# A new written order, new loads and new PSUM banks for an attention + ELU feed-forward kernel; the first pair's q and k transposed as fp32

## The chip, the cores and the metric

The kernel runs on one core of one Trainium2 chip, in one launch. The time is the device time of that core in microseconds (us), as the median of several executions. The core has five engines that run side by side and wait for each other through semaphores: TensorE (PE, matmuls; PEld is its weight load), VectorE (DVE), ScalarE (ACT), GpSimd (POOL) and SyncE (SP). Transfers between memory and the core are issued by POOL, SP and ACT into queues.

## The reference

Attention over 8 batches of 8 heads, 576 positions, 64 dimensions, and behind it a feed-forward block with ELU over all 4608 tokens:

```python
scores = scale * np.matmul(q, k.transpose(0, 1, 3, 2))
mask_local = (rel >= 0) & (rel < stride)                  # stride = 32, rel = i - j
mask_strided = (rel >= 0) & (pos[None, :] % stride == pos[:, None] % stride)
masks = np.stack([mask_local if h < H // 2 else mask_strided for h in range(H)], axis=0)
attn = softmax(np.where(masks, scores, -1e9))             # over the last axis
x = (attn @ v) as 4608 tokens x 512                       # 8 heads x 64 beside each other
h = x @ w_in                                              # 512 -> 2048
g = np.where(h > 0, h, np.exp(np.minimum(h, 0)) - 1)
return g @ w_out                                          # 2048 -> 512, fp32
```

Heads 0 to 3 are local, heads 4 to 7 strided. Inputs and output are fp32 in memory; the matmuls run in bf16.

## The kernel before, in words

The work of each engine follows one text, `ORDER` (line 36), in which each word is one step. A loop at the end of the kernel reads the words and calls the function of each; every engine then works through its own steps in the order of the text and waits only where a semaphore says so. The words:

- `w.bank.n.n...` (`warm`, L385): matmuls on zeros with n columns each, into a bank whose content is not needed. They keep TensorE busy where it would wait.
- `D.x.b` (`load`): a load, issued by POOL. `qs`, `ks`, `vs` are the strided heads of batch b, `ql`, `kl`, `vl` the local ones, `wi0` to `wi3` the quarters of w_in (4 of 16 blocks m of 128 hidden columns each), `wo0` to `wo3` those of w_out. Loads convert to bf16. From the ninth load on, each one waits until the eighth before it has landed, because eight semaphores are reused in turn.
- `K`, `k` (`cast`, L390): half of the first strided pair's q or k from fp32 to bf16. This pair comes through SP's and ACT's queues instead of POOL's, as fp32, into a staging space that lies in `g`.
- `T` (`transposes`, L401, L408, L411): q or k of a pair of heads of batch 0 or 1 is transposed by TensorE into a PSUM bank; `c` (VectorE) or `C` (ScalarE) (`copy_T`) copies it out. A pair is named by batch, kind and number: `0s0` is the first strided pair of batch 0, `1l1` the second local one of batch 1. For `0s0` the transpose goes in halves, `.0` and `.1`.
- `X` (`dma_T`, L601): from batch 2 on, q and k are transposed by a DMA that SP issues.
- `S` (`scores`, L453), `e` (`exp_s`, L460, ScalarE), `m` (`mask`, L467 and L473, VectorE), `O` (`pv`: values and row sums; L480 to L501 in an old form for batches 0 and 1, L516 and L523 in a new one from batch 2), `n` (logarithm of the sums, L551, ScalarE), `r` (exponential of its negative, L556, ScalarE), `x` (`write_x`, L581, VectorE: the product goes to `xT` as bf16): the attention steps of a pair's half.
- `V`, `W`: copies that bring v into the form that `O` reads. `F`: fills of masks and ones.
- `L.ch.m.bank` (L608): the first product for a chunk of 512 tokens and block m, four matmuls of 512 columns over the four blocks of 128 features. Features 0 to 255 come from local heads, 256 to 511 from strided ones. For chunk 0 it is split: `a` does the strided two, `b` the local two.
- `h` (exponential, L616, ScalarE), `i` (L625, VectorE) or `j` (L623, ScalarE) (the clamp), `g` (L636 or L634, VectorE): the ELU of a block; `g` reads the PSUM bank last, which is then free.
- `Z.ch.k.part.bank` (L642): a quarter of the second product of 128 tokens, four matmuls; `q` (VectorE) or `o` (ScalarE) copies the finished bank out (L648), and `t` stores it from SP's queue, `u` from SP's and ACT's in turn.
- `Y`, `y` (L672, L682): the last tile in three pieces, each stored as soon as it is ready.

PSUM has eight banks; the last number in a word that writes PSUM names them, so the text also fixes which step waits for which bank.

TensorE's front, before: zeros, transposes of `0s0` in halves as the casts finish, the other pairs' transposes, scores, PV, each with zeros between them; then four `a` of quarter 1 (blocks 5, 7, 4, 6), a transpose of batch 1 (`T.1s1.q`), and the `b` of these blocks. From there on the dense words of a chunk alternate with the attention words of a later batch. At the end only `Z` words are left.

Of the kernel before, what the change touches and what calls it, by code (L numbers as in the profile page):

```python
# [8 lines left out]
F32 = mybir.dt.float32  # L9
BF16 = mybir.dt.bfloat16  # L10
I32 = mybir.dt.int32
ALU = mybir.AluOpType
# [3 lines left out]
S = 576  # L16
# [24 lines left out]
D.wi2.0 c.0l0.q n.0s0.0 w.4.314 S.0l1.1.45 S.0l1.0.23 m.0s0.1 F.mk r.0s0.0 T.0l0.k.7 O.0s0.1.60 e.0l1.1  # L41
x.0s0.0 D.wo0.0 F.ml e.0l1.0 w.0.224.224.102 O.0s1.1.15 c.0l0.k n.0s0.1 D.wo1.0 w.4.247 O.0s1.0.43
n.0s1.1 m.0l1.0 n.0s1.0 r.0s1.1 D.ql.1 w.2.512.512.108 S.0l0.0.23 x.0s1.1 e.0l0.0 V.0 w.7.512.331
S.0l0.1.01 r.0s1.0 m.0l1.1 r.0s0.1 w.7.512 O.0l1.0.75 m.0l0.0 e.0l0.1 O.0l1.1.32 x.0s1.0 n.0l1.0 m.0l0.1
w.2.224.224 O.0l0.0.10 n.0l1.1 x.0s0.1 r.0l1.0 w.1.142 O.0l0.1.54 r.0l1.1 x.0l1.0 D.ks.1 n.0l0.0
w.4.224.224 a.0.5.6 x.0l1.1 n.0l0.1 a.0.7.7 r.0l0.0 a.0.4.0 r.0l0.1 x.0l0.0 a.0.6.4 D.kl.1 x.0l0.1
T.1s1.q.3 b.0.5 c.1s1.q b.0.7 h.0.5 b.0.4 h.0.7 i.0.5 b.0.6 h.0.4 g.0.5 T.1s0.q.5 D.wo2.0 a.0.12.3
C.1s0.q i.0.4 a.0.13.6 h.0.6 g.0.4 a.0.14.5 b.0.12 a.0.15.2 h.0.12 b.0.15 j.0.6 D.vs.1 a.0.2.1 j.0.12
b.0.13 g.0.6 b.0.2 h.0.13 g.0.12 a.0.1.4 h.0.2 i.0.7 b.0.1 i.0.13 a.0.3.3 g.0.7 h.0.1 D.wo3.0 b.0.3
i.0.2 b.0.14 h.0.3 g.0.2 a.0.0.7 j.0.1 b.0.0 a.0.11.1 g.0.1 h.0.0 a.0.10.0 h.0.14 D.vl.1 i.0.0 b.0.10  # L50
j.0.3 g.0.0 b.0.11 h.0.10 a.0.8.4 g.0.3 b.0.8 h.0.11 g.0.13 Z.0.0.0.7 h.0.15 i.0.10 D.ks.2 i.0.14
Z.0.0.1.7 h.0.8 g.0.10 j.0.11 Z.0.3.0.6 j.0.15 g.0.11 D.vs.2 Z.0.3.1.6 g.0.15 g.0.14 a.0.9.3 D.qs.2
i.0.8 b.0.9 g.0.8 Z.0.1.0.5 h.0.9 j.0.9 T.1s0.k.4 D.kl.2 Z.0.1.1.5 C.1s0.k g.0.9 T.1s1.k.2 S.1s0.1.01
c.1s1.k T.1l1.k.4 e.1s0.1 T.1l1.q.3 c.1l1.k T.1l0.q.2 S.1s1.0.01 m.1s0.1 Z.0.3.2.6 e.1s1.0 C.1l1.q
m.1s1.0 Z.0.1.2.5 C.1l0.q O.1s1.0.43 T.1l0.k.2 n.1s1.0 S.1s1.1.01 c.1l0.k Z.0.0.2.7 e.1s1.1 r.1s1.0
# [12 lines left out]
Z.1.2.1.2 n.2s0.1 x.2s1.1 Z.1.3.2.7 r.2s0.1 m.2s0.0 O.2s1.0.01 x.2s0.1 Z.1.2.2.2 n.2s1.0 O.2s0.0.34
r.2s1.0 Z.1.3.3.7 n.2s0.0 x.2s1.0 Z.1.2.3.2 r.2s0.0 q.1.3 S.2l0.0.01 S.2l0.1.56 x.2s0.0 Z.1.1.0.7
e.2l0.0 q.1.2 e.2l0.1 m.2l0.0 S.2l1.0.01 S.2l1.1.34 X.qs.3 Z.1.1.1.7 m.2l0.1 e.2l1.0 e.2l1.1 m.2l1.0  # L70
O.2l0.0.56 O.2l0.1.01 X.kl.3 n.2l0.0 m.2l1.1 Z.1.0.0.4 n.2l0.1 Z.1.0.1.4 r.2l0.0 t.1.3 O.2l1.1.23
r.2l0.1 x.2l0.0 Z.1.0.2.4 n.2l1.1 x.2l0.1 O.2l1.0.56 r.2l1.1 Z.1.0.3.4 X.ql.3 n.2l1.0 x.2l1.1 Z.1.1.2.7
r.2l1.0 D.qs.4 Z.1.1.3.7 x.2l1.0 D.kl.4 q.1.0 L.2.11.6 W.3 S.3s0.0.01 S.3s0.1.23 h.2.11 L.2.3.5 e.3s0.1
i.2.11 g.2.11 L.2.7.4 D.ks.4 h.2.3 o.1.1 D.vl.3 i.2.3 L.2.2.6 m.3s0.1 e.3s0.0 g.2.3 L.2.5.7 h.2.7 h.2.2
i.2.7 L.2.4.5 h.2.5 g.2.7 j.2.2 i.2.5 L.2.9.3 m.3s0.0 h.2.4 D.vs.4 g.2.5 L.2.0.4 h.2.9 g.2.2 j.2.4
D.ql.4 L.2.14.7 i.2.9 h.2.0 g.2.4 O.3s0.1.01 h.2.14 g.2.9 L.2.10.6 n.3s0.1 i.2.0 L.2.6.5 i.2.14 h.2.10
g.2.0 r.3s0.1 L.2.8.3 i.2.10 X.ks.4 g.2.14 h.2.6 L.2.13.4 x.3s0.1 h.2.8 j.2.6 g.2.10 O.3s0.0.01 X.qs.4
L.2.1.7 n.3s0.0 i.2.8 g.2.6 L.2.15.6 r.3s0.0 g.2.8 t.1.0 h.2.1 L.2.12.5 x.3s0.0 h.2.15 X.kl.4 i.2.1
S.3s1.0.01 S.3s1.1.23 g.2.1 e.3s1.1 Z.2.1.0.7 e.3s1.0 m.3s1.1 i.2.15 h.2.13 m.3s1.0 S.3l0.0.01
# [70 lines left out]
def kernel(  # L150
# [583 lines left out]
```

## Time and profile before

| | us |
|---|---|
| median of 3 runs (lowest to highest) | 305.96 (305.51 to 306.67) |
| the profiled execution, its own time | 306.22 |
| its span, first to last instruction | 304.5 |
| TensorE busy | 297.1 |
| ScalarE busy | 228.5 |
| VectorE busy | 226.2 |
| GpSimd busy | 80.2 |
| first dense matmul starts | 18.62 |

The granted clock of TensorE is 1.00 over the whole span. In the lines shown below, times count from the first instruction. A line of a timeline gives start, length, engine, line of the kernel, operation, what it writes and reads, how many are merged, and in brackets how long the engine was idle before and what ended that. The matmuls are pipelined, so the length of one is longer than the distance to the next.

### The profile page before, as it was taken

To read this page: it belongs to the slowest core of one execution; us is meant where nothing else is said; L and a number is where in the kernel's file an instruction comes from. 1 tells how busy PE (TensorE), PEld (TensorE's weight loads), DVE (VectorE), ACT (ScalarE), POOL (GpSimd) and SP (SyncE) were. 2 spreads that over 40 slices of the span, in tenths; PEclk is the share of its full clock that TensorE was granted. 3 is DMA by queue.
4 is the path that set the end of the run, shared out by engine and by line. 5 is a ranking of instruction groups with operands and counts; after the bars stand their busy time and mean duration, and the time that the engine had idled before them with its cause. 6 is when DMAs were issued, how large, how long until landed. Compare 5 with 4: busy or idle time off the path is not lost.

```text
span 304.5 us, 6258 instructions
## 1 busy us (share of the span) xinstructions
PE 297.1 (98%) x2339; PEld 146.8 (48%) x2339; DVE 226.2 (74%) x435; ACT 228.5 (75%) x412; POOL 80.2 (26%) x110
## 2 busy tenths in 40 slices
PE   6999999999999999999999999999999999999994
PEld 2654455445544454445544554445444544444444
DVE  6777968798779978896788878976788358895020
ACT  4778678598879888997989889978777559982101
POOL 8922436830471008530188250000000000000000
PEclk9999999999999999999999999999999999999999
DMA  8999999999899759999899499801120022000053
GB/s 165 190 206 207 207 193 169 169 198 204 158 158 168 128 123 134 162 192 171 196 154 154 61 132 149 195 16 56 38 69 0 2 69 69 2 1 0 4 155 119
DMA packets 107358, 37.63 MB, mean 124 GB/s; under 512 B 89152, under 2 KB 102848, under 8 KB 107328
## 3 DMA queue, kind: packets, MB, share of 16 engines
q0 software_dynamic: 69728, 19.47, 62.3%
q1 hardware_dynamic: 36920, 17.08, 28.4%
q10 hardware_dynamic: 680, 0.69, 0.8%
q8 instruction: 18, 0.29, 0.4%
q14 instruction: 12, 0.10, 0.1%
HBM read 39.53 MB, written 9.44 MB: 161 GB/s over the span
## 4 chain that ended last, share of the span: by engine, by line
PE 86%; DVE 6%; ACT 3%; issue 2%; DMA 2%; ACTq 0%; DVEq 0%
PE ps L642 40%; PE ps L608 33%; PE ps L453 4%; DVE g L636 3%; DVE he L625 2%; PE ps L523 2%; PE ps L516 2%; DMA g<-in_k_dram 2%; PE ps L385 1%; PE ps L672 1%; ACT he L616 1%; PE ps L411 1%; PE ps L496 1%; PE ps L480 1%; ACT ln L551 0%
## 5 line engine op out<-in xcount | busy, mean ns | idle before, releaser
L642 PE MATMUL ps<-w_out_sb,g 128*128 128x512 bf16 x560 | 132.8, 379 | 0.5 <-DVE g L636 0.5
L608 PE MATMUL ps<-xT,w_in_sb 128*128 128x512 bf16 x576 | 130.5, 379 | 0.2 <-DVE g L634 0.2
L616 ACT ACTIVATE he<-ps 128x512 f32<-128x512 f32 x144 | 80.9, 596 | 22.2 <-PE ps L608 20.0
L608 PEld LDWEIGHTS <-w_in_sb 128*128 128x128 bf16 x576 | 55.0, 98 | 64.3 <-issue 1.1
L642 PEld LDWEIGHTS <-g 128*128 128x128 bf16 x560 | 51.1, 98 | 55.7 <-issue 0.8
L636 DVE TENSOR_TENSOR g<-he,ps 128x512 bf16<-128x512 bf16 x92 | 62.0, 684 | 1.9
L581 DVE TENSOR_TENSOR xT<-ps,ln 64x576 bf16<-64x576 f32 (+1 forms) x64 | 42.6, 678 | 20.3 <-ACT ln L556 19.4
L460 ACT ACTIVATE e<-ps 72x576 bf16<-72x576 f32 (+1 forms) x64 | 39.1, 647 | 12.7 <-PE ps L453 11.9
L625 DVE TENSOR_SCALAR he<-he 128x512 bf16<-128x512 f32 x92 | 40.2, 446 | 7.5 <-ACT he L616 6.8
L551 ACT ACTIVATE ln<-ps 64x576 f32<-64x576 f32 (+1 forms) x64 | 36.3, 583 | 10.0 <-PE ps L523 5.0
L634 DVE SCALAR_TENSOR_TENSOR g<-he,ps 128x512 bf16<-128x512 bf16 x52 | 34.8, 682 | 7.2 <-ACT he L623 6.9
L556 ACT ACTIVATE ln<-ln 64x576 f32<-64x576 f32 (+1 forms) x64 | 38.5, 619 | 1.2
L623 ACT ACTIVATE he<-he 128x512 bf16<-128x512 f32 x52 | 32.5, 630 | 1.3 <-DVE g L636 0.8
L648 DVE COPY osb<-ps 128x512 f32<-128x512 f32 x22 | 15.1, 685 | 16.3 <-PE ps L642 16.0
L243 POOL DMA_DIRECT2D ql<-in_q_dram x24 | 20.1, 840 | 7.7 <-DMA vl<-in_v_dram 4.1
L648 ACT COPY osb<-ps 128x512 f32<-128x512 f32 x13 | 7.6, 586 | 17.9 <-PE ps L642 14.1
L250 POOL DMA_DIRECT2D kl<-in_k_dram x24 | 17.8, 747 | 11.4 <-DMA w_out_sb<-in_moe_w_out_dram 3.7
L473 DVE TENSOR_TENSOR pm<-e,mask_l 128x576 bf16<-128x576 bf16 x32 | 14.1, 453 | 6.9 <-ACT e L460 5.3
L467 DVE TENSOR_TENSOR pm<-e,mask_s 72x576 bf16<-72x576 bf16 x32 | 14.2, 451 | 4.3 <-ACT e L460 4.1
L260 POOL DMA_DIRECT2D vl<-in_v_dram x8 | 9.8, 1220 | 9.5 <-PE ps L523 7.2
L233 POOL DMA_DIRECT2D vs<-in_v_dram x8 | 5.2, 652 | 25.6 <-DVE vsp L588 24.7
L516 PEld LDWEIGHTS <-vsp 72*128 72x128 bf16 x192 | 9.1, 98 | 5.5 <-issue 0.4
(93 smaller groups left out, 153.2 us busy)
## 6 DMA issues: line engine op xcount, KB each, us to landing
out_dram<-osb SPq DMA_DIRECT2D x30, 144.0 KB
vl<-in_v_dram POOLq DMA_DIRECT2D x8, 288.0 KB, 8.9
w_in_sb<-in_moe_w_in_dram POOLq DMA_DIRECT2D x4, 512.0 KB, 13.1
w_out_sb<-in_moe_w_out_dram POOLq DMA_DIRECT2D x4, 512.0 KB, 16.8
kl<-in_k_dram POOLq DMA_DIRECT2D x24, 72.0 KB, 7.3
ql<-in_q_dram POOLq DMA_DIRECT2D x24, 72.0 KB, 8.4
ks<-in_k_dram POOLq DMA_DIRECT2D x5, 320.0 KB, 8.2
vs<-in_v_dram POOLq DMA_DIRECT2D x5, 320.0 KB, 9.1
```

The lines of the kernel that those rows point to most:

```text
L460: nc.scalar.activation(e[0:R], tiles.pop(("S", key, u))[0:R], ACT.Exp, scale=scale)
L551: nc.scalar.activation(t, s_ps, ACT.Ln)
L556: nc.scalar.activation(t, t, ACT.Exp, scale=-1.0)
L581: nc.vector.tensor_mul(dst, o_ps, rc)
L608: nc.tensor.matmul(tiles["h", ch, m], lhsT=w_in_sb[:, c, m * 128:(m + 1) * 128], rhs=xT[:, c, ch * CHUNK:(ch + 1) * CHUNK], start=(c == 2) ...
L616: nc.scalar.activation(e, tiles["h", i[0], i[1]], ACT.Exp)
L623: nc.scalar.activation(e1, e, ACT.Relu, bias=1.0, scale=-1.0)
L625: eng.tensor_scalar(e1, e, scalar1=1.0, scalar2=1.0, op0=ALU.min, op1=ALU.subtract)
L634: nc.vector.scalar_tensor_tensor(dst, e1, -1.0, h, op0=ALU.mult, op1=ALU.max)
L636: nc.vector.tensor_tensor(dst, e1, h, op=ALU.max)
L642: nc.tensor.matmul(ops, lhsT=g[ch % 2][:, m, kk * 128:(kk + 1) * 128], rhs=w_out_sb[:, m, :], start=(m == 0), stop=(m == MC - 1), skip_gro ...
L648: eng(o_sb, tiles.pop(("o", int(ch), int(kk))))
```

## The change

The order text is written anew: other places for nearly all words, other banks, other blocks first, and another split of copies and clamps between VectorE and ScalarE at single places (18 `q` and 17 `o` for 22 and 13 before, while 92 `i` and 52 `j` stay). The code changes with it in these points:

- The casts `K` and `k` are gone. The halves of pair `0s0` are transposed straight from the fp32 staging space, with a second identity in fp32 (72 x 72), into PSUM as fp32; the copy out of PSUM converts.
- The scores of `0s0` load 72 weight columns instead of 128.
- `load` can take a quarter of w_in in two halves; the new text does not use it.
- In front, the order of loads behind the first pair is kl, kl, ql, ql, vs, vs, vl, then w_in quarters 3, 0, 2, 1, then qs of batch 1, w_out 0, ks of batch 1, and so on. Before, it was ql, kl, ql, vs, kl, vs, vl, w_in 1, qs of batch 1, w_in 3, 0, 2.
- For batch 2, ql (four loads) is loaded ahead of qs and kl.
- O of `0l0.0` comes after the first two `a`. Five `a` (blocks 15, 12, 14, 13, 1) stand before the first `b`.
- Chunk 6's second product is spread between the first products of chunks 7 and 8.
- One late tile is stored from two queues (`u.8.2`), where there were two (`u.8.3`, `u.7.2`).

```diff
-w.7.512.512.512.512.512.512.512.512 D.ql.0.1 F.vp D.kl.0.1 F.v1 D.ql.0.0 k.q.0 F.ms D.vs.0.0 T.0s0.q.0.7
-D.kl.0.0 K.q.1 K.k.1 D.vs.0.1 K.k.0 C.0s0.q.0 w.0.512.512.512.512.512 T.0s0.k.0.6 D.vl.0 T.0s0.k.1.5
-T.0s0.q.1.4 c.0s0.k.0 T.0s1.k.7 c.0s0.k.1 c.0s1.k w.0.324 T.0s1.q.6 c.0s0.q.1 D.wi1.0 S.0s0.0.01 c.0s1.q
-S.0s0.1.23 e.0s0.0 w.5.185 S.0s1.0.45 D.qs.1 S.0s1.1.67 e.0s1.0 m.0s0.0 w.2.224.224 T.0l1.k.1 D.wi3.0
-e.0s1.1 m.0s1.0 w.0.499 T.0l0.q.0 C.0l1.k D.wi0.0 m.0s1.1 T.0l1.q.7 e.0s0.1 c.0l1.q w.4.155 O.0s0.0.16
...
+w.7.512.512.512.512.512.512.512.512 D.kl.0.1 F.vp D.kl.0.0 F.ms D.ql.0.1 F.v1 D.ql.0.0 T.0s0.q.0.7
+D.vs.0.1 T.0s0.k.0.6 c.0s0.q.0 D.vs.0.0 C.0s0.k.0 D.vl.0 w.0.512.512.512.512.512.394 T.0s1.k.7
+T.0s0.q.1.6 c.0s1.k S.0s0.0.01 c.0s0.q.1 e.0s0.0 w.2.269 T.0s1.q.5 D.wi3.0 T.0s0.k.1.7 C.0s1.q m.0s0.0
+w.2.421 T.0l1.k.6 c.0s0.k.1 D.wi0.0 S.0s1.1.01 C.0l1.k S.0s1.0.23 S.0s0.1.45 D.wi2.0 T.0l0.k.7 e.0s1.1
+w.2.123 T.0l1.q.6 e.0s1.0 D.wi1.0 m.0s1.1 e.0s0.1 w.0.224.224.182 T.0l0.q.1 m.0s1.0 D.qs.1 c.0l0.k
+C.0l1.q w.0.512.132 O.0s1.1.05 F.mk O.0s1.0.43 n.0s1.1 S.0l1.0.67 D.wo0.0 F.ml e.0l1.0 w.2.198
...
+m.0l1.1 r.0s0.1 n.0l1.0 w.4.224.224.105 O.0l1.1.51 x.0s0.1 n.0l0.1 m.0l0.0 D.wo2.0 n.0l1.1 a.0.15.6
+r.0l1.1 a.0.12.3 r.0l1.0 x.0l1.1 O.0l0.0.21 r.0l0.1 x.0l1.0 a.0.14.0 n.0l0.0 x.0l0.1 a.0.13.7 r.0l0.0
+x.0l0.0 D.vs.1 a.0.1.1 b.0.15 b.0.12 b.0.13 h.0.12 b.0.1 h.0.13 a.0.0.2 h.0.15 D.wo3.0 a.0.2.5 i.0.13
...
+o.8.0 t.8.0 Z.8.1.3.2 Z.7.1.2.5 q.8.1 Z.7.1.3.5 t.8.1 Z.7.0.2.4 q.7.1 Z.7.0.3.4 t.7.1 Y.7.3.0.7 o.7.0
+t.7.0 y.7.3.0 Y.7.3.1.6 y.7.3.1 Y.7.3.2.5 y.7.3.2
...
+    identity_f = consts.tile([RS, RS], F32, tag="identity_f", name="identity_f")
...
-        if y is not None:
+        if y is not None and nm != "wi":
...
+            cs = slice(0, KC) if y is None else (slice(2, KC), slice(0, 2))[int(y)]
+            nc.gpsimd.dma_start(out=w_in_sb[:, cs, i * 512:(i + 1) * 512],
+                                in_=w_in_v[:, cs, i * 512:(i + 1) * 512])
...
+    nc.vector.memset(identity_f, 1.0)
...
+    nc.gpsimd.affine_select(
+        identity_f, identity_f, compare_op=ALU.is_equal, fill=0.0,
+        base=0, pattern=[[1, RS]], channel_multiplier=-1)
...
-    def cast(eng, nm, i):
-        n, f = "qk".index(nm), 2 * NS * D
-        eng(half(raw[nm + "s"][0:RS, 0:f], int(i)), half(stage[0:RS, n * f:(n + 1) * f], int(i)))
...
-        t = ps[:, bank, :].bitcast(BF16)[:, 0:S // (1 + len(part))]
+        t = ps[:, bank, 0:W] if part else ps[:, bank, :].bitcast(BF16)[:, 0:S]
...
+            n = "qk".index(nm) * 2 * NS * D
+            src = stage[0:RS, n:n + 2 * NS * D].rearrange("p (h f) -> p h f", h=2)
...
-                nc.tensor.transpose(t[:, i * RS:(i + 1) * RS], src[:, P.head(x), c0:c0 + 2 * D],
-                                    identity[0:RS, 0:RS])
+                nc.tensor.transpose(t[:, i * RS:(i + 1) * RS], src[:, x, c0:c0 + 2 * D], identity_f)
...
-                nc.tensor.matmul(dst, lhsT=P.kT[pr, k0:k0 + 128], rhs=rhs, start=True, stop=True,
+                n = RS if key == "0s0" else 128
+                nc.tensor.matmul(dst[0:n], lhsT=P.kT[pr, k0:k0 + n], rhs=rhs, start=True, stop=True,
...
```

More of the change, by code (lines that the diff above doesn't have):

```diff
@@ L41 @@
[L41 to L55, printed above, removed]
@@ L273, in load @@
             i = int(what[2])
-            nc.gpsimd.dma_start(out=w_in_sb[:, :, i * 512:(i + 1) * 512],
-                                in_=w_in_v[:, :, i * 512:(i + 1) * 512])
+            cs = slice(0, KC) if y is None else (slice(2, KC), slice(0, 2))[int(y)]
+            nc.gpsimd.dma_start(out=w_in_sb[:, cs, i * 512:(i + 1) * 512],
+                                in_=w_in_v[:, cs, i * 512:(i + 1) * 512])
         elif nm == "wo":
@@ L686 @@
     run = {
-        "w": warm, "K": lambda nm, x: cast(nc.vector.tensor_copy if nm == "q" else nc.scalar.copy, nm, x),
-        "k": lambda nm, x: cast(nc.scalar.copy if nm == "q" else nc.vector.tensor_copy, nm, x), "T": transposes, "F": fill,
+        "w": warm, "T": transposes, "F": fill,
         "c": lambda *a: copy_T(nc.vector.tensor_copy, *a),
```

189 lines of the change are left out of this document (99 added, 90 removed).

## The prediction

> **What bounds the kernel now.** I read the page first, then each engine's busy time in stretches of 10 us, then the timelines of the front by engine, then the chain of waits and the end. Columns of a group: busy us, mean ns of one, idle us before it.
>
> ```profile
> PE 297.1 (98%) x2339; PEld 146.8 (48%) x2339; DVE 226.2 (74%) x435; ACT 228.5 (75%) x412; POOL 80.2 (26%) x110
> ...
> L642 PE MATMUL ps<-w_out_sb,g 128*128 128x512 bf16 x560 | 132.8, 379 | 0.5 <-DVE g L636 0.5
> L608 PE MATMUL ps<-xT,w_in_sb 128*128 128x512 bf16 x576 | 130.5, 379 | 0.2 <-DVE g L634 0.2
> ...
> L608 PEld LDWEIGHTS <-w_in_sb 128*128 128x128 bf16 x576 | 55.0, 98 | 64.3 <-issue 1.1
> ```
>
> TensorE is the bound: it is busy 98% of the span, and its 1136 dense matmuls waited 0.7 us in all. So there are only three places where a new order can change the time: the front, before dense work runs; the few stalls inside; the end behind the last matmul.
>
> ```profile
> core 0 of [0], span 304.5 us
> core 0: us, PE busy (x) PEld busy (x) DVE busy (x) ACT busy (x) POOL busy (x), PEclk, DMA share, GB/s
> 60.00:70.00 10.00, 9.78 (x74) 4.49 (x73) 9.70 (x20) 9.24 (x19) 3.62 (x5) 1.00 1.57 193
> 90.00:100.00 10.00, 9.91 (x60) 4.72 (x59) 9.85 (x20) 9.51 (x18) 2.61 (x4) 1.00 1.80 168
> 100.00:110.00 10.00, 9.53 (x99) 4.89 (x97) 8.49 (x17) 9.07 (x17) 0.00 (x0) 1.00 0.46 95
> 150.00:160.00 10.00, 9.94 (x71) 4.42 (x69) 8.82 (x17) 8.32 (x16) 7.60 (x11) 1.00 1.08 152
> ```
>
> These four (with the length of each first) are the only stretches from 40 us to 300 us in which TensorE is under 10.00. They lack 0.22, 0.09, 0.47 and 0.06, so 0.84 us in all, and the three worst lie where VectorE is at 9.7 and 9.85 of 10, or just behind. All of the middle can yield 0.84 us and no more.
>
> ```profile
> 1.26 3.50 PE L385 MATMUL ps<-zero 128*128 128x512 bf16 x8 [1.26 <-DVE zero L303]
> 4.95 0.30 PE L401 MATMUL ps<-identity,qs 72*128 72x72 bf16 x4 [0.19 <-ACT qs L390]
> 5.09 1.25 PE L385 MATMUL ps<-zero 128*128 128x512 bf16 x5
> 7.26 0.43 PE L401 MATMUL ps<-identity,ks 72*128 72x72 bf16 x8 [0.92 <-ACT ks L390]
> ...
> 18.62 1.89 PE L608 MATMUL ps<-xT,w_in_sb 128*128 128x512 bf16 x8
> 20.35 0.42 PE L408 MATMUL ps<-identity,xT 72*128 72x72 bf16 x8
> 20.75 1.89 PE L608 MATMUL ps<-xT,w_in_sb 128*128 128x512 bf16 x8
> ```
>
> In this timeline of TensorE (start, length, instruction, idle before) the first dense matmul starts at 18.62. The 8 at 18.62 are first halves of chunk 0 (tokens `a`, strided heads), those at 20.75 begin the second halves (`b`, local heads). Up to there TensorE fills waits with matmuls on zeros, so it is ScalarE that sets the front:
>
> ```profile
> 8.76 0.65 ACT L460 ACTIVATE e<-ps 72x576 bf16<-72x576 f32 x1 [1.26 <-PE ps L453]
> 9.69 1.18 ACT L460 ACTIVATE e<-ps 72x576 bf16<-72x576 f32 x2 [0.28 <-PE ps L453]
> 10.76 0.63 ACT L429 COPY kTl<-ps 128x576 bf16<-128x576 bf16 x1
> 11.28 0.66 ACT L460 ACTIVATE e<-ps 72x576 bf16<-72x576 f32 x1
> ...
> 19.27 0.76 ACT L556 ACTIVATE ln<-ln 128x288 f32<-128x288 f32 x2
> ```
>
> Its first exponential is at 8.76, and its last reciprocal ends at 20.03; a multiply of 0.46 on VectorE then lets the `b` start at 20.75. One 576-wide instruction occupies 0.53 (10.76 less 9.69, halved). From the slot after the fourth exponential (11.28 + 0.55 = 11.83) to 20.03 stand 4 exponentials, 8 logarithms and 8 reciprocals, 8.20 us with little idle in them.
>
> **The change, part by part.** *No casts.* Three casts of ScalarE and one of VectorE go; the 16 transposes of the first pair read the fp32 loads. The 0.92 us that TensorE waited for a cast go too, but filler stands in their place: the columns of zeros are 12,946 for 12,903 before, by the order text, so TensorE's own time in front is as it was.
>
> *What a transpose in fp32 costs* no row shows. The row at 4.95, with the next start at 5.09, gives 0.035 each in bf16, the lower end. [...] I take 0.13, nearest to the two rows added, so 0.53 for a group of four. [...]
>
> *The front, worked through.* Zeros end at 4.76. Then q and k of half 0: 1.06, to 5.82; zeros of 2954 columns (5.77 matmuls at 0.216): 1.25, to 7.07. Then the transposes of the loaded `ks`:
>
> ```profile
> 2.13 0.64 POOL L233 DMA_DIRECT2D ks<-in_k_dram  x1
> ```
> ```profile
> ks<-in_k_dram POOLq DMA_DIRECT2D x1, 160.0 KB, 5.1
> ```
>
> The second row is the load's issue with its median time to landing: it lands at 2.13 + 5.1 = 7.23. So 0.26 to 7.50, q of half 1 to 8.03, the first scores (0.24, and 0.1 for the switch) to 8.37, and ScalarE's first exponential at 8.45, 0.3 sooner than 8.76. But the new order gives ScalarE three 576-wide copies between the exponentials (of q of pair 0s1, k and q of 0l1) where there was one. It copies until 9.5, waits for TensorE's k of half 1 and the transposes of 0l1 to 9.85, copies to 10.37, has three exponentials to 12.0 and the last copy to 12.53. The old 8.20 us follow: 20.73. With the multiply, the `b` start at 21.25. The new order has done five `a` by then instead of four and a transpose, 0.43 less 0.26, so 20.75 corresponds to 20.93: the front is 0.3 us later. With 0.035 a transpose ScalarE ends near 20.1 and the front is bounded by weights instead.
>
> *Weights in another order* (w_in quarters 3, 0, 2, 1, and qs of batch 1 behind them). POOL's loads wait for the eighth before them to land, so its rows give the landings:
>
> ```profile
> 17.86 0.64 POOL L233 DMA_DIRECT2D xT<-in_k_dram  x1 [2.95 <-DMA w_in_sb<-in_moe_w_in_dram]
> 19.46 0.64 POOL L233 DMA_DIRECT2D xT<-in_k_dram  x1 [0.96 <-DMA xT<-in_q_dram]
> 22.39 0.75 POOL L278 DMA_DIRECT2D w_out_sb<-in_moe_w_out_dram  x1 [2.29 <-DMA w_in_sb<-in_moe_w_in_dram]
> 24.54 0.65 POOL L233 DMA_DIRECT2D g<-in_v_dram  x1 [1.41 <-DMA w_in_sb<-in_moe_w_in_dram]
> 27.08 0.75 POOL L278 DMA_DIRECT2D w_out_sb<-in_moe_w_out_dram  x1 [1.89 <-DMA w_in_sb<-in_moe_w_in_dram]
> ```
>
> A quarter takes 2.15 to 2.93, so the second now lands at 17.86 plus that, 20.0 to 20.8. The fifth `a` needs it, so the `b` cannot start before 20.45 to 21.2. That holds the front between -0.5 and +0.3 even where ScalarE is early. The fourth quarter lands by 25.5; the first `a` that reads it stands 5.6 us behind the fifth, at 26: no wait, by half a microsecond.
>
> *Order in the middle.* The counts are the same (92 clamps on VectorE, 52 on ScalarE, 64 of each attention step); four PSUM copies go from VectorE to ScalarE. What a switch costs shows here, in the chain of waits:
>
> ```profile
> 75.49 1.73 PE ps L642 x8
> 77.22 0.36 PE ps L453 x12
> 77.58 0.97 PE ps L642 x4
> ```
>
> Four dense matmuls take 0.97 behind scores, where eight took 1.73 (0.86 for four): 0.1 on the way out, and about as much on the way in. By the order texts dense work now breaks off 35 times for scores, transposes or the old PV form, for 33 before: two more at 0.2, of which one only moves over from the front: +0.2. The stalls of 0.84 may go or double; stretches with VectorE near its limit stand in both orders (by token counts and row durations, about 9.4 and 9.9 us of work in 10 at the same two places, and a new one in chunk 6), so I take them as they are, 0, with -0.84 and +1.0 for the range. Bank reuse is no tighter: spans under 2.6 us from a first product to its bank's next use are 14 in both.
>
> *The end.*
>
> ```profile
> 300.66 0.29 DVE osb L682
> ```
>
> The last tile still goes out in pieces; the last 128-column copy and its store remain, from 300.66 to 304.5. One full tile before them goes through one queue instead of two, and is done well before: 0.
>
> *Sum.* +0.3 + 0.2 + 0 = +0.5 on 306.22 us, the time of the profiled execution (span 304.5, and 1.72 around it): 306.7. The median shown is 305.96, 0.26 lower, so 306.5 for the median.
>
> **The rivals.** [...]
>
> *Late loads* (slower). qs of batch 2 is now issued behind its four ql loads:
>
> ```profile
> 50.10 2.74 SPq L601 DMA_TRANSPOSE qTs<-qs  x1
> ```
> ```profile
> 64.49 0.44 PE L453 MATMUL ps<-qTs,kTs 64*128 64x72 bf16 x16
> ```
>
> That moves this transpose by about 2 us, to 52, and its scores from 64.5 to 62.3: the 14 us between them shrink to 10. Elsewhere TensorE's work between a transpose and its use comes to 11 us or more. If one of them, or a quarter of w_in, is over its margin by 1.5 to 3 us: 307.5 to 309. Against it: the queue's order is by need, and each margin is positive.
>
> *Clean* (faster). All 0.84 us of stalls go, quick transposes let ScalarE end near 19.9 and w_in lands at its fastest: -0.5, so -1.34: 304.6, just within 0.5%; a little off the end as well makes it faster. For it: nothing of the work grew. Against it: three mild gains at once.
>
> *No effect where it is meant*: the casts are gone, but copies take their room on ScalarE. That is the forecast itself.
>
> **How the numbers follow.** Under 0.5%, 1.5 us, this kernel's runs (305.51 to 306.67) hardly tell a change from none. Forecast 0.62 (306.5; its own range 305.4 to 307.4), slow transposes 0.13, late loads 0.12, clean 0.13, of which 0.11 over the bound. So faster 0.11, same 0.64, slower 0.25. The range reaches down past most of the clean case, 304.8, and up into the two slow ones, 308.3.
>
> **What would show it.** The fp32 transposes' start-to-start (0.13); the first exponential near 8.45; ScalarE's last reciprocal near 20.7; the `b` near 21.2; stretches below 10.00 in the middle that add up to about 0.8; the end from the last copy still 3.8. The prediction is wrong if TensorE waits on a DMA in the middle, or if the front moved by over a microsecond.

## The result, and the profile after

| | before | after |
|---|---|---|
| median of 14 runs each (lowest to highest) | 305.85 (305.51 to 306.67) | 306.86 (306.40 to 308.59) |
| the profiled execution, its own time | 306.22 | 306.81 |
| its span | 304.5 | 305.1 |
| second halves of chunk 0 (`b`) start | 20.75 (as 20.93 in the new order) | 21.92 |
| from the last copy to the end | 3.84 | 3.83 |

The ratio of after to before is 1.0037, with a 95% interval of 1.0027 to 1.0047: one microsecond slower. Before's profiled execution lay 0.37 over its kernel's median, after's 0.05 under its own, so the two profiles differ by only 0.6. Most line numbers move by 4 to 6: `L391` are the zeros, `L405` the fp32 transposes, `L457` the scores, `L612` and `L646` the dense products. Of casts_back, a run further down, two of the seven executions lie near 314 us and are left out of its ratio, and the profiled one is one of these two.

The page of after, its engines and the two dense groups:

```profile
PE 297.6 (98%) x2345; PEld 147.7 (48%) x2345; DVE 220.1 (72%) x429; ACT 231.7 (76%) x415; POOL 80.2 (26%) x111
...
L646 PE MATMUL ps<-w_out_sb,g 128*128 128x512 bf16 x560 | 134.1, 379 | 0.0
L612 PE MATMUL ps<-xT,w_in_sb 128*128 128x512 bf16 x576 | 131.8, 379 | 0.4
```

The dense products waited 0.4 us instead of 0.7. TensorE is as busy as before; VectorE has lost 6 us of work, ScalarE has gained 3. After in stretches of 10 us, the only four below 10.00 between 40 and 300:

```profile
core 0: us, PE busy (x) PEld busy (x) DVE busy (x) ACT busy (x) POOL busy (x), PEclk, DMA share, GB/s
...
50.00:60.00 10.00, 9.76 (x76) 4.76 (x74) 7.58 (x18) 7.39 (x17) 1.46 (x3) 1.00 2.01 135
...
100.00:110.00 10.00, 9.94 (x99) 5.11 (x100) 8.60 (x18) 8.22 (x15) 0.00 (x0) 1.00 1.35 198
110.00:120.00 10.00, 9.84 (x81) 4.99 (x80) 6.31 (x10) 9.01 (x15) 3.61 (x5) 1.00 0.39 71
...
160.00:170.00 10.00, 9.85 (x80) 4.71 (x78) 9.85 (x20) 9.23 (x17) 5.00 (x7) 1.00 2.21 154
```

They lack 0.61 us, where before lacked 0.84. The end is unchanged: the last copy (timeline of VectorE in after) starts 3.83 before the span's end.

```profile
301.27 0.29 DVE L686 COPY osb<-ps 128x128 f32<-128x128 f32 x1 [0.55 <-PE ps L676]
```

So the loss lies in the front. After's timeline of TensorE:

```profile
4.46 0.67 PE L405 MATMUL ps<-identity_f,g 72*128 72x72 f32 x8
4.97 1.41 PE L391 MATMUL ps<-zero 128*128 128x512 bf16 x6
7.22 0.43 PE L411 MATMUL ps<-identity,ks 72*128 72x72 bf16 x8 [0.84 <-DMA ks<-in_k_dram]
7.49 0.45 PE L405 MATMUL ps<-identity_f,g 72*128 72x72 f32 x4
7.87 0.33 PE L457 MATMUL ps<-qTs,kTs 64*72 64x72 bf16 x8
...
15.76 0.22 PE L457 MATMUL ps<-qTl,kTl 64*128 64x96 bf16 x2
16.82 0.26 PE L457 MATMUL ps<-qTl,kTl 64*128 64x96 bf16 x4 [0.84 <-issue]
17.01 0.35 PE L391 MATMUL ps<-zero 128*128 128x224 bf16 x2
...
20.38 6.88 PE L612 MATMUL ps<-xT,w_in_sb 128*128 128x512 bf16 x30
```

Three things are to be seen. Eight fp32 transposes take 4.97 less 4.46, so 0.064 each. The wait for a cast (0.92 us) is gone, and a wait of nearly the same length for the load of `ks` (0.84) stands in its place. And at 15.98, in the middle of the scores of `0l0.0`, TensorE stands still for 0.84 us "<-issue", that is, for nothing that the profile shows: two of the six matmuls of this step had run, and the program has no wait between them.

ScalarE in after, from its first exponential to its last reciprocal of batch 0:

```profile
8.24 0.65 ACT L464 ACTIVATE e<-ps 72x576 bf16<-72x576 f32 x1 [2.67 <-PE ps L457]
...
11.81 0.62 ACT L428 COPY qTl<-ps 128x576 bf16<-128x576 bf16 x1
12.46 0.41 ACT L555 ACTIVATE ln<-ps 128x288 f32<-128x288 f32 x1
13.13 0.65 ACT L464 ACTIVATE e<-ps 128x576 bf16<-128x576 f32 x1 [0.25 <-DVE mask_l L360]
...
17.40 0.65 ACT L464 ACTIVATE e<-ps 128x576 bf16<-128x576 f32 x1 [0.52 <-DVE xT L585]
...
20.49 0.41 ACT L555 ACTIVATE ln<-ps 128x288 f32<-128x288 f32 x1
20.93 0.44 ACT L560 ACTIVATE ln<-ln 128x288 f32<-128x288 f32 x1
```

It starts 0.5 sooner than before (8.76) and ends 1.3 later (20.03). The last exponential, at 17.40, comes 0.04 us behind the end of the two zero matmuls that stand behind the scores of `0l0.0` (17.01 and 0.35 long, so 17.36), which go to the free columns of a bank that these scores use. It is so in casts_zeros, too (zeros to 17.09, exponential at 17.13), while in no_late_fill, which leaves these zeros out, it comes 0.04 behind the scores themselves (17.49 and 17.53). So it seems to wait for the zeros, 0.28 us longer than for the scores. The chain of waits in after, from the standstill to the `b`:

```profile
15.98 0.84 issue
16.82 0.26 PE ps L457 x4
17.08 0.28 PE ps L391 x2
...
19.11 0.97 PE ps L612 x4
20.07 0.24 PE ps L500 x2
20.32 0.15 PE ps L505 x6
20.46 0.02 issue
20.49 0.42 ACT ln L555
...
21.41 0.47 DVE xT L585
...
21.92 2.10 PE ps L612 x9
```

Up to 20.46 it runs through TensorE: scores, zeros, PV, and at 19.11 the four matmuls of the two `a` that the new order puts ahead of the last PV. Behind that it runs through ScalarE and VectorE. ScalarE has no idle time over 0.04 from 17.40 on either, so both engines are without slack up to 20.49.

### The profile page after: what moved, and what is told of

Same layout as the page of the kernel before. It is cut to its first block, busy times and chain, and to the rows that moved or that the text cites. A ratio compares the mean times of both kernels' runs of the same rounds, so it can differ in the third digit from the quotient of the medians.

```text
span 305.1 us, 6265 instructions
## 1 busy us (share of the span) xinstructions
PE 297.6 (98%) x2345; PEld 147.7 (48%) x2345; DVE 220.1 (72%) x429; ACT 231.7 (76%) x415; POOL 80.2 (26%) x111
## 3 DMA queue, kind: packets, MB, share of 16 engines
q1 hardware_dynamic: 37004, 17.23, 31.3%
## 4 chain that ended last, share of the span: by engine, by line
PE 87%; DVE 6%; ACT 2%; issue 2%; DMA 2%; POOL 0%; DVEq 0%; POOLq 0%
PE ps L646 39%; PE ps L612 35%; PE ps L457 4%; PE ps L527 2%; DVE g L640 2%; PE ps L520 2%; DMA ks<-in_k_dram 2%; PE ps L391 1%; DVE xT L585 1%; PE ps L676 1%; DVE he L629 1%; ACT e L464 1%; DVE g L638 1%; ACT ln L555 1%; PE ps L411 1%
## 5 line engine op out<-in xcount | busy, mean ns | idle before, releaser
L646 PE MATMUL ps<-w_out_sb,g 128*128 128x512 bf16 x560 | 134.1, 379 | 0.0
L612 PE MATMUL ps<-xT,w_in_sb 128*128 128x512 bf16 x576 | 131.8, 379 | 0.4
L612 PEld LDWEIGHTS <-w_in_sb 128*128 128x128 bf16 x576 | 54.8, 98 | 64.3 <-issue 1.1
L646 PEld LDWEIGHTS <-g 128*128 128x128 bf16 x560 | 50.8, 98 | 54.2 <-issue 0.2
L629 DVE TENSOR_SCALAR he<-he 128x512 bf16<-128x512 f32 x92 | 38.9, 436 | 9.4 <-ACT he L620 8.6
L652 DVE COPY osb<-ps 128x512 f32<-128x512 f32 x18 | 12.2, 687 | 15.2 <-PE ps L646 14.1
L652 ACT COPY osb<-ps 128x512 f32<-128x512 f32 x17 | 9.9, 585 | 15.3 <-PE ps L646 15.2
L234 POOL DMA_DIRECT2D qs<-in_q_dram x7 | 4.9, 695 | 28.6 <-DMA qTs<-qs 27.1
```

Source lines behind the costliest of these rows:

```text
L612: nc.tensor.matmul(tiles["h", ch, m], lhsT=w_in_sb[:, c, m * 128:(m + 1) * 128], rhs=xT[:, c, ch * CHUNK:(ch + 1) * CHUNK], start=(c == 2) ...
L629: eng.tensor_scalar(e1, e, scalar1=1.0, scalar2=1.0, op0=ALU.min, op1=ALU.subtract)
L646: nc.tensor.matmul(ops, lhsT=g[ch % 2][:, m, kk * 128:(kk + 1) * 128], rhs=w_out_sb[:, m, :], start=(m == 0), stop=(m == MC - 1), skip_gro ...
L652: eng(o_sb, tiles.pop(("o", int(ch), int(kk))))
```

## The experiments

Twelve kernels were run, four at a time on one chip, each against the kernel before on that chip (305.85 to 305.88 us). The first questions were where the microsecond lies, and what the standstill is: TensorE out of instructions (A), a wait in the scores that the profile does not see (B), or ScalarE's longer chain with the standstill beside it.

**old_front_new_rest.** The front as it was, with the weights loaded in the new order, and everything behind it in the new order.

```diff
 (the text of before up to x.0l0.1, with its loads in the new order, then the text of after)
-a.0.5.6 ... a.0.7.7 ... a.0.4.0 ... a.0.6.4
+a.0.15.6 ... a.0.13.7 ... a.0.14.0 ... a.0.12.3
```

> The front of the kernel before (casts, its order, banks and zeros, up to the last multiply of batch 0), with the loads in the changed kernel's order and the blocks 15, 13, 14, 12 first; from there on the changed kernel's order. If the loss is in the front and the middle gained (traces: front +1.0, middle -0.4): 305.5 to 305.7, faster than both. If the new middle depends on its own front: 306.3 or more. If front and middle were told apart wrongly, and the middle holds the loss: 306.8.

Measured: 305.81 us, ratio 1.0000 (0.9991 to 1.0009). The new order behind the front neither costs nor gains more than the 0.3 us of the interval; the microsecond comes with the new front. After's profile is 0.4 quicker behind the front than before's, which fits the 0.37 by which before's profiled execution lies over its median.

**split_fill.** After's 2954 zero columns behind the first transposes in matmuls of 128 instead of 512 columns, 18 more matmuls and as many weight loads.

```diff
-w.0.512.512.512.512.512.394
+w.0.128.128. ... .128.10
```

> The changed kernel, with the 2954 columns of zeros ahead of the third transpose cut into 24 matmuls (23 of 128 and one of 10) instead of 6: the same TensorE time within 0.05 us, but 36 more TensorE instructions early on. Theory A (TensorE ran out of instructions: in the changed kernel its instruction queue fetched 16 KB from 14.19 to 15.47, and it stood still from 15.98 to 16.82 in the middle of the scores of 0l0.0 with no wait on record): the standstill moves about 36 instructions forward, to the scores of 0l0.1 or next to them, near 14 to 15.5 us; none is left at the scores of 0l0.0. Time 306.2 to 307.0. Theory B (the third matmul of these scores waits for data or for a bank): a standstill of about 0.8 us stays between the second and third matmul of the scores of 0l0.0, time 306.9. Theory C (it was a chance of one execution): no standstill anywhere, 306.3.

Measured: 307.16 us (1.0049, 1.0035 to 1.0064). The standstill in the scores of `0l0.0` is gone, though nothing was done to that step, so B falls. But it did not move to another place, as A had it: TensorE stands nowhere without a cause in this execution, and the time is over all three forecasts. And the front hardly got shorter: the first exponential came at 8.50, because `ks` landed 0.26 later, the last reciprocal ended at 21.26, and the `b` started at 21.80, 0.12 sooner than in after. Another wait had come in place of the standstill: `vl` landed at 16.18 instead of 15.02, and VectorE's copy of it waited 0.61 us for that.

**no_fill.** All zeros of after left out behind the first eight.

```diff
-w.0.512.512.512.512.512.394 ... w.4.224.224.105
```

> The changed kernel without the zeros behind the first eight: 33 matmuls, some 3.7 us of TensorE's time and 66 instructions of the front go. Theory A (instructions): the whole front lies within what is fetched at first, the next fetch falls among dense matmuls, no standstill; if ScalarE's chain is what is left, the second halves of chunk 0 start at 21.2 as predicted instead of 21.92, time 306.2. Theory D (TensorE's own place in the order sets the front, filler included): they start up to 1.5 us sooner, 305.4. Theory E (the zeros keep the clock up): TensorE's matmuls of the front and the first dense ones run at half clock (0.43 us a dense matmul instead of 0.216), time over 308.

Measured: 308.82 us (1.0089, 1.0070 to 1.0109). In stretches:

```profile
4.00:10.00 6.00, 4.45 (x82) 3.55 (x80) 3.35 (x11) 2.26 (x5) 6.00 (x10) 0.96 1.17 190
10.00:20.00 10.00, 8.59 (x145) 6.34 (x142) 7.06 (x19) 9.12 (x22) 5.43 (x9) 0.51 1.50 187
20.00:30.00 10.00, 9.95 (x52) 4.61 (x53) 6.54 (x14) 7.19 (x16) 2.90 (x4) 1.00 1.24 207
```

The granted clock is 0.51 from 10 to 20 us, with TensorE busy for 8.59 of the 10, where before and after have 1.00: here the zeros do keep the clock up. ScalarE's first exponential (8.14) and the end of its last reciprocal (21.38) stand where they stood, without a standstill, but two things changed at once: 3.7 us of zeros went, and TensorE ran at half speed. With them ScalarE waits for TensorE's last PV:

```profile
20.50 0.41 ACT L553 ACTIVATE ln<-ps 128x288 f32<-128x288 f32 x1 [0.39 <-PE ps L498]
```

So this run does not tell whether TensorE's speed sets the front. The profiled execution, 306.97, is the fastest of six by 1.5 us; what the other five lost, no trace shows.

**casts_back** and **casts_zeros.** The casts put back into after; then the same with two of the zero matmuls moved to where TensorE waits for the casts.

```diff
+k.q.0 ... K.k.0 ... K.q.1 K.k.1          (casts_back)
-w.7.512 (8 times) ... w.0.512.512.512.512.512.394
+w.7.512 (9 times) ... w.5.512 ... w.0.512.512.512.394   (casts_zeros, besides)
```

> The changed kernel with the fp32 transposes undone: the casts of pair 0s0 to bf16 stand before them again, three on ScalarE and one on VectorE, and the transposes are bf16. My step: ScalarE has nothing else to do before 8.2, and the first scores wait for the transposes of ks, which lands at 7.2, so the casts cost nothing: first exponential at 8.1 to 8.4 (8.24 with fp32), time 306.9 within 0.3. Rival (the fp32 transposes are what makes the front late): the second halves start 0.3 to 0.6 us sooner, 306.4. Other rival (the fp32 path gains time): the first exponential is 0.5 later or more, 307.4.

> The changed kernel with the casts put back (the run casts_back), and of its zeros two matmuls of 512 columns moved: one ahead of the first transposes, one between q's and k's transposes, so that TensorE has work while the casts run; the sum of zeros is the same. If casts_back was 1 us slower because TensorE's idle time of 0.34 and 0.1 at 4.8 to 5.7 us held the clock at half, the clock rises by 5.8 us in every execution here, the time is 306.9 within 0.3, and no execution lies near 314. If the casts themselves cost it, on ScalarE or by their place in the queue, the time stays at 307.9.

Measured: casts_back 307.94 us (1.0064, 1.0051 to 1.0078), against the expectation; casts_zeros 306.89 (1.0037, 1.0020 to 1.0055), as after and as expected. The timelines of TensorE, casts_back and then casts_zeros:

```profile
5.19 0.42 PE L406 MATMUL ps<-identity,qs 72*128 72x72 bf16 x4 [0.34 <-ACT qs L395]
5.71 0.42 PE L406 MATMUL ps<-identity,ks 72*128 72x72 bf16 x4
5.94 2.66 PE L390 MATMUL ps<-zero 128*128 128x512 bf16 x6
```
```profile
5.09 0.43 PE L407 MATMUL ps<-identity,qs 72*128 72x72 bf16 x4
5.33 0.62 PE L391 MATMUL ps<-zero 128*128 128x512 bf16 x1
5.74 0.45 PE L407 MATMUL ps<-identity,ks 72*128 72x72 bf16 x4
5.99 1.22 PE L391 MATMUL ps<-zero 128*128 128x512 bf16 x4
```

In casts_back the six zeros take 0.43 to 0.44 each, where matmuls of 512 columns at full pace start 0.216 apart (the dense ones at 20.38 in after): in this execution TensorE kept half its pace until 27.7 us. The profile's granted clock reads 1.00 there all the same, so the pace is read from the rows. TensorE had paused for 0.34 us ahead of q's transposes and for 0.1 again ahead of k's. In casts_zeros no pause stands there, and the pace doubles at 6.5. So with the pauses filled, casts and fp32 transposes are worth the same in the new order (306.89 and 306.86): the first point of the change moves the time by nothing. A pause alone is not the whole cause, though: old_front_new_rest pauses for 0.36 us at the same place and its pace doubles at 5.7. And what the other five executions of casts_back (307.35 to 308.26) lose against casts_zeros, no trace shows.

**copies_dve.** The two additional copies of ScalarE in after moved to VectorE.

```diff
-C.0s1.q ... C.0l1.q
+c.0s1.q ... c.0l1.q
```

> The changed kernel with two PSUM copies of the front, q of pair 0s1 and q of pair 0l1, on VectorE instead of ScalarE; nothing else moves. If ScalarE's chain from its first exponential to its last reciprocal of batch 0 sets the front (13.13 us in the changed kernel, 11.28 before), it loses two instructions of 0.53: the last reciprocal ends at 20.3 to 20.6 instead of 21.37, the second halves start at 20.9 to 21.2 instead of 21.92, and the time is 305.9 to 306.3. If the front is set by TensorE's standstill or by loads, the second halves stay at 21.9 and the time at 306.9. If VectorE cannot take the copies without delaying the masks, ScalarE's gain comes back as idle time and the time is 306.6 or more.

Measured: 306.97 us (1.0033, 1.0021 to 1.0046), no gain. ScalarE in copies_dve:

```profile
8.24 0.65 ACT L463 ACTIVATE e<-ps 72x576 bf16<-72x576 f32 x1 [2.13 <-PE ps L456]
9.57 0.64 ACT L431 COPY kTl<-ps 128x576 bf16<-128x576 bf16 x1 [0.68 <-DVE pm L470]
...
12.63 0.41 ACT L554 ACTIVATE ln<-ps 128x288 f32<-128x288 f32 x1 [0.58 <-PE ps L483]
13.47 0.65 ACT L463 ACTIVATE e<-ps 128x576 bf16<-128x576 f32 x1 [0.43 <-PE ps L456]
```

ScalarE's 1.05 us of copies came back as idle time: 1.96 us between first exponential and last reciprocal, for 1.06 in after. The last reciprocal ended at 21.22. So these two instructions are not what sets the front; this run stands still, too, and behind the standstill its order is after's.

**no_late_fill.** After without its last three groups of zeros. By the order text these are seven matmuls with 1356 columns, not the 1107 of the expectation, so 0.57 us at 0.216 for 512.

```diff
-w.0.224.187 ... w.6.224.168 ... w.4.224.224.105
```

> The changed kernel without its last three groups of zeros (1107 columns, 0.46 us at full clock), which stand between the last scores and the first dense matmuls. If ScalarE sets the front, these zeros stand in time that TensorE has to wait anyway: last reciprocal at 21.2 to 21.5, second halves at 21.8 to 22.0, time 306.9 within 0.2. If TensorE's own work sets it, everything behind comes 0.46 sooner: 306.4. If the clock falls for want of work, it is slower than 307.2.

Measured: 306.51 us (1.0029, 1.0012 to 1.0045), 0.35 under after's median, with intervals that overlap; its profiled execution, 307.25, is a long one of its own (`ks` landed late, the standstill ended at 17.23). Its last reciprocal ends 4.22 us behind the end of the standstill, where it is 4.55 in after: the 0.28 by which the last exponential waits for zeros is gone. By the median, too, zeros of after stand in the way a little behind the standstill.

**The instruction fetch.** The page of after has two DMA queues of the kind "instruction". One, q8, moved 18 packets of 16 KB in the whole run; that it is TensorE's is an inference from what follows. Times of its first packet, in us, beside the 445th TensorE instruction of the trace (matmuls and weight loads counted in order of start). The last column gives the kernel's median and the execution that the row is from; fewer_instr and the rows below it are of kernels described further down.

| kernel | first packet | 445th instruction | `vl` landed | last exponential starts | last reciprocal ends | median (this execution) |
|---|---|---|---|---|---|---|
| before | 13.88 to 14.86 | 16.26 | 13.97 | 16.80 | 20.04 | 305.85 (306.22) |
| old_front_new_rest | 13.73 to 14.71 | 16.30 | 14.20 | 16.84 | 20.08 | 305.81 (305.83) |
| after | 14.19 to 15.48 | 16.82, after 0.84 idle | 15.02 | 17.40 | 21.37 | 306.86 (306.81) |
| copies_dve | 13.45 to 15.33 | 16.68, after 0.36 idle | 15.19 | 17.26 | 21.22 | 306.97 (306.68) |
| casts_zeros | 13.83 to 15.19 | (448th) 16.56, after 0.50 idle | 14.88 | 17.13 | 21.09 | 306.89 (306.81) |
| no_late_fill | 14.12 to 15.80 | 17.23, after 0.89 idle | 15.35 | 17.53 | 21.45 | 306.51 (307.25) |
| split_fill | 12.13 to 13.31 | 14.98 | 16.18 | 17.34 | 21.26 | 307.16 (307.23) |
| no_fill | 13.91 to 15.27 | 18.34 | 15.54 | 16.98 | 21.38 | 308.82 (306.97) |
| fewer_instr | 14.24 to 15.36 | 17.01 | 16.11 | 17.46 | 21.39 | 306.96 (306.65) |
| fewer_copy_dve | 14.24 to 15.44 | 17.15 | 15.46 | 17.31 | 21.24 | 306.81 (306.28) |
| fp32_in_before | 12.76 to 14.20 | 15.88 | 15.95 | 17.10 | 20.34 | 306.75 (306.03) |
| split_before | 12.82 to 13.79 | 15.08 | 14.94 | 16.87 | 20.11 | 306.39 (306.45) |
| fp32_fewer | 13.87 to 15.69 | 17.52 | 16.82 | 17.98 | 21.21 | 306.48 (307.71) |

Four kernels in the new order stop at the 445th to 448th instruction, and go on 1.34 to 1.43 us behind the end of the packet. Counted with the semaphore instructions and the drain that the trace lists for TensorE (five in after, two in casts_zeros), the stop is in all four ahead of the 450th. The kernels without a stop reach that place as late or later: in before the 445th starts 1.40 behind the packet, so before just clears it. split_before, on before's front, holds at the same count for 0.13 us, up to 15.21, 1.42 behind its packet: its six scores at 15.08 take 0.42 us instead of 0.30. So theory A fits in this form: in none of the 13 kernels of the table does TensorE get past the 448th instruction sooner than 1.34 us behind the end of the packet. In 13 of the 14 kernels (no_fill is the other) the third packet starts between the 696th and the 717th instruction. In before and in after it is at the 708th, and the eighteenth at the 4488th, so 252 recorded instructions for a packet in the mean, with steps of 175 to 395 in after. What sets the place of the stop, no run shows.

What the stop costs is another question. The `b` start at 21.64 to 22.00 in the four profiles of the new front with the stop, and at 21.78 to 21.94 in the four without it (split_fill, no_fill, fewer_instr, fewer_copy_dve), where other waits came in its place. What all eight share stands behind the last exponential: from its start to the end of the last reciprocal it is 3.23 or 3.24 us in all five kernels with before's front, and 3.92 to 3.97 in the eight with the new one, except no_fill at half pace (4.40). No run changes the order there.

**fp32_in_before.** The fp32 transposes alone, in before's order.

```diff
-k.q.0 ... K.q.1 K.k.1 ... K.k.0
```

> The kernel before, in its own order of everything, with one part of the change alone: the first pair's q and k transposed as fp32, and the three casts of ScalarE and the one of VectorE left out. If fp32 transposes are as cheap as the changed kernel's rows say (0.064 each) and ScalarE sets the front, the first exponential comes at 8.2 to 8.4 instead of 8.76, the last reciprocal at 19.5 to 19.7, the second halves start at 20.2 to 20.4 instead of 20.75, and the time is 305.4 (-0.4). If the casts only filled time in which ScalarE waited and w_in bounds the front behind it, nothing changes: 305.85. If the transposes cost more than they show, it is slower: 306.2 or more.

Measured: 306.75 us (1.0028, 1.0015 to 1.0040), slower than before. The first exponential comes at 8.23, half a microsecond sooner, as expected. TensorE is thus further in its instructions, the packet comes at 12.76 instead of 13.88, among the small packets of the load of `vl`, and `vl` lands at 15.95 instead of 13.97. Of the 2304 packets of 128 bytes of this load the last starts at 13.61 in before, ahead of the instruction packet; here 52 start behind 14.00, the last at 14.90. VectorE, and POOL behind its reused semaphore, wait for it:

```profile
15.97 0.55 DVE L588 COPY vl<-vl 32x1472 bf16<-32x1472 bf16 x1 [0.71 <-DMA vl<-in_v_dram]
```
```profile
16.23 0.65 POOL L233 DMA_DIRECT2D xT<-in_q_dram  x1 [1.95 <-DMA vl<-in_v_dram]
```

The profiled execution, 306.03, is the fastest of the twelve, so these rows show a wait that came with the change, and not how the median's 0.87 us are made up.

**split_before** tests this on the kernel before, with nothing changed but the number of instructions.

```diff
-w.0.512.512.512.512.512
+w.0.128.128. ... .128        (20 times)
```

> The kernel before with one edit: its five zero matmuls of 512 columns behind the first transposes are made 20 of 128 columns, so TensorE has 30 more instructions (15 matmuls and their weight loads) and the same columns. Theory F: the fetch of TensorE's instructions (one packet of 16 KB) is asked for at a fixed place in its instruction stream, so it comes sooner, falls into the 2304 small packets of batch 0's `vl` load on one DMA engine, and `vl` lands at 14.8 to 16.2 instead of 13.97; VectorE's copy of `vl` waits for it where it is behind 15.7, and the time is 306.2 to 306.8. If instruction count has nothing to do with it, `vl` lands at 14.0 within 0.3 and the time is 305.9 within 0.2.

Measured: 306.39 us (1.0029, 1.0012 to 1.0045), `vl` at 14.94, the packet at 12.82. POOL's row in split_before, where before's row (14.26, no wait) stands in the prediction:

```profile
15.23 0.65 POOL L233 DMA_DIRECT2D xT<-in_q_dram  x1 [0.81 <-DMA vl<-in_v_dram]
```

The packet comes a microsecond sooner and `vl` lands one later, as expected. That the small packets share one DMA engine, no trace shows. Thirty more instructions for the same columns cost half a microsecond in the median. Part of the expectation failed: in the profiled execution (306.45) VectorE did not wait for `vl`, and the `b` start only 0.08 later than before's, so where the rest of the 0.5 goes is not shown.

**fp32_fewer.** fp32_in_before with five zero matmuls less.

```diff
-w.0.324 ... w.5.185 ... w.2.224.224 ... w.4.155
```

> As the run fp32_in_before (fp32 transposes in the order of before), with five zero matmuls left out ahead of the `vl` load's end (1112 columns, 10 instructions). Theory F: the instruction fetch comes later than its 12.76, by the 10 instructions, 0.2 to 0.6 us, so `vl` lands at 14.5 to 15.5 instead of 15.95 and the copy of `vl` waits less; last reciprocal at 19.8 to 20.1, time 305.9 to 306.3 against 306.75. If the fetch does not move, `vl` lands at 15.9 again and the time is 306.7.

Measured: 306.48 us (1.0036, 1.0014 to 1.0059), from 305.86 to 309.82. The packet did move, to 13.87, but took 1.82 there, and `vl` landed at 16.82 in the profiled execution, over a microsecond later than expected. That execution (307.71) is a long one, and its pace doubled at 7.2 us only. In it, fewer instructions moved the collision and did not make it go away; the median, 0.27 under fp32_in_before's, does not tell the two apart.

**fewer_instr** and **fewer_copy_dve.** After with 14 TensorE instructions less ahead of the scores of `0l0.0`; then one copy on VectorE and the zeros ahead of the first PV left out, too. The merged zeros go to banks 5 and 0 and overwrite values there that are still in use, so part of the output differs; the instructions are all there.

```diff
-w.2.224.224.122 ... w.1.224.224.224.117 ... w.6.224.224.224.224
+w.5.512.58 ... w.0.512.277
-C.0l1.q w.0.512.132      (fewer_copy_dve, besides)
+c.0l1.q
```

> The changed kernel with 14 TensorE instructions fewer ahead of the scores of 0l0.0: one group of four zero matmuls left out (896 columns, 0.37 us), two groups put together into 512-column matmuls on other banks. Theory F: TensorE cannot go past about its 445th recorded instruction before 1.35 us behind the end of its fetch (16.8), and in the changed kernel that place lay inside the scores of 0l0.0; now it lies behind them, so the exponential of 0l0.0 starts at 16.8 to 17.0 instead of 17.40 with no idle time of 0.52, the last reciprocal ends at 20.8 to 21.0, the second halves start at 21.3 to 21.5, and the time is 306.4 (-0.5). If the standstill belongs to those scores and not to the count, it stays ahead of them and the time is 306.9. If the missing zeros let the clock fall, it is 307.5 or more.

> As the run fewer_instr, and the copy of q of pair 0l1 on VectorE instead of ScalarE, with the 644 zeros left out that stand on TensorE ahead of the first PV product. If ScalarE's number of instructions is the rest of the loss, it ends 0.3 to 0.5 sooner than in fewer_instr: last reciprocal at 20.3 to 20.6, second halves at 20.9 to 21.1, time 306.0. If TensorE's instructions or VectorE's masks come last instead, it is as fewer_instr or slower: 306.4 or more.

Measured: 306.96 us (1.0040, 1.0025 to 1.0055) and 306.81 (1.0038, 1.0022 to 1.0054). The standstill is gone from the scores, as expected of the count. The gain is not there. The edit made waits of its own; TensorE in fewer_instr:

```profile
14.99 0.49 PE L390 MATMUL ps<-zero 128*128 128x512 bf16 x2 [0.47 <-DVE xT L584]
15.42 0.30 PE L456 MATMUL ps<-qTl,kTl 64*128 64x96 bf16 x6
15.72 0.31 PE L483 MATMUL ps<-pm,ones 72*64 72x288 bf16 x2
15.87 0.30 PE L492 MATMUL ps<-pm,vs 72*64 72x72 bf16 x8
16.46 0.30 PE L456 MATMUL ps<-qTl,kTl 64*128 64x96 bf16 x6 [0.30 <-ACT e L463]
```

The zeros now wait for bank 0 (0.47), the scores behind them for the exponential that frees it (0.30), and the exponential of `0l0.0` starts at 17.46. Besides, `ks` landed 0.33 later than in after, and VectorE's copy of `vl` waited 0.46. So what the standstill alone costs after is not isolated. By its rows it is at most the 0.52 us of ScalarE's wait, 0.28 of them behind zeros. The rest goes with the new front's order, most of it behind the last exponential, and which part of that order costs it remains open. No kernel tried beats before; old_front_new_rest equals it.

## Why the prediction was right, and where it was not

The time, 306.86, is 0.36 over the 306.5 forecast, inside the range of 304.8 to 308.3 and inside "no change" at 0.5%. That it lies so near is luck in part: errors of opposite sign made it up. By the prediction's own signs of being wrong it just passes: the front moved by 0.99, where over a microsecond was the sign, and TensorE waits for no load in the middle.

*Transposes in fp32.* The 0.13 each of the sum was an estimate, the 0.035 of a bf16 transpose and the 98 ns of a weight load added up (both rows of before), and no run shows it: in after they took 0.064, 1.8 times the 0.035. After lists 16 weight loads of 0.142 for them, each beside the transpose ahead of it. The slow transposes, to which the forecast gives a chance of 0.13, did not come.

*First exponential and copies.* Predicted 8.45, with the last copy ending at 12.53; measured 8.24, and the slot behind the copy begins at 12.46. Right, and the price of the transposes hardly mattered to it: TensorE waited for `ks`, which was to land at 7.23 and released it at 7.22.

*"The old 8.20 us follow: 20.73."* This is the step that failed. From 12.46 to the last reciprocal's end at 21.37 it is 8.91. The 8.20 held 0.34 of idle time; the 8.91 hold 0.77, of which 0.52 stand behind the standstill, and the remaining 0.28 go with logarithms and reciprocals that stand alone instead of in pairs. I had carried over a duration from another order, with that order's pairs and without a standstill of TensorE, and did not look for what limits TensorE's supply of instructions, though the page of before lists q8 with its 18 packets. The front was predicted at +0.3 and came out at 21.92 against 20.93, +1.0.

*Weights.* The second quarter was to land at 20.0 to 20.8 and the fourth by 25.5. POOL in after waits for them:

```profile
20.70 0.65 POOL L234 DMA_DIRECT2D g<-in_v_dram  x1 [1.80 <-DMA w_in_sb<-in_moe_w_in_dram]
...
25.79 0.65 POOL L234 DMA_DIRECT2D xT<-in_k_dram  x1 [1.76 <-DMA w_in_sb<-in_moe_w_in_dram]
```

The landings are 20.42 and 25.51; TensorE waits for neither.

*Middle.* Switches at +0.2 and stalls at 0 were predicted; old_front_new_rest measures 0.0 for both together. That the switches cost nothing is not shown: the stalls are 0.23 less in after's profile, which would hide a cost of that size. The late-loads rival falls: TensorE's only waits for a load in after are those in front, at 7.22. *Clean* falls, too: stalls of 0.61 remain.

*End.* Predicted unchanged, 3.83 measured against 3.84.

*Sum.* Front +0.7 more than predicted, middle 0.2 less, and the median of before 0.1 under the one shown: +0.4. In the pair of profiles the difference is 0.59 against +0.5 predicted, and that agreement is luck: before's profiled execution was a long one.

## What to carry to other kernels

When a front is written anew, add up the waits as well as the instructions: a chain's duration from the old order cannot be carried over, since each engine's idle time belongs to its order (8.20 us with 0.34 idle came out as 8.91 with 0.77). When a standstill disappears, look whether the chain got shorter: here another wait came in its place each time. Look at the instruction queue's packets in the DMA part of the page, and count matmuls and weight loads up to the place where TensorE stopped here, the 445th to 448th: small fillers and an earlier start can cost more than they bring while loads are under way (30 more instructions came with 0.5 us more in split_before, a first exponential at 8.23 instead of 8.76 with 0.9 us more in fp32_in_before). And take the difference of two profiles only after placing each in the scatter of its kernel's runs.

## What was not expected of the hardware

TensorE stood still for 0.36 to 0.89 us at one count of instructions, the 445th to 448th of the trace, and went on 1.34 to 1.43 us behind the end of a 16 KB instruction packet. That packet took 0.97 to 1.88 us while loads were under way. Where it came sooner or took longer than in before, `vl` landed later, by up to 2.85 us (at 13.97 in before, 14.94 in split_before, 15.95 in fp32_in_before, 16.82 in fp32_fewer).

And in the traced execution of casts_back TensorE kept half its pace until 27.7 us; it took 7 us longer than that of casts_zeros (313.76 and 306.81). In before, too, the eight zeros at 1.26 take 0.44 each, half the full pace, though the granted clock reads 1.00 over the whole span, from 0 to 4 us, too: it says nothing of the time ahead of the first rise. In the other kernels here the rise comes at 4.1 to 7.2 us with TensorE at work from 1.26, so 2.8 to 6.0 behind its start. What sets that time, no run shows. Why one kernel with two short pauses missed the rise for 20 us, and others with pauses of 0.36 and 0.62 us (old_front_new_rest, split_before) did not, remains open.
